# Attention scores as four 64x64 array tiles at a time, mask and row maximum in one VectorE instruction, strided heads first, k loads from ScalarE's queue

## The chip, the cores and the metric

The kernel runs on one core of one Trainium2 chip. The metric is the device time of one execution in microseconds. The kernel before takes 834.89 us (median of three runs, 834.66 to 837.99).

## The reference, cut to what matters

Three layers follow each other. Banded attention over 4 batches, 8 heads, 576 positions and 64 channels gives 2304 rows of 512 numbers; a mixture of 8 experts (top 1) works on these rows; a rational-function feed-forward layer ends it. The change is in the attention alone:

```python
scores = scale * np.matmul(q, k.transpose(0, 1, 3, 2))
mask_plain = (rel >= 0) & (rel < window)                                            # heads 0 to 3, window 32
mask_dil = (rel >= 0) & (rel < window * dilation) & (rel % dilation == 0)           # heads 4 to 7, dilation 4
scores = np.where(masks[None, :, :, :], scores, -1000000000.0)
scores = scores - np.max(scores, axis=-1, keepdims=True)
attn = np.exp(scores)
attn = attn / (np.sum(attn, axis=-1, keepdims=True) + 1e-09)
return np.matmul(attn, v)
```

## The kernel before, in words

A unit is one head of two batches; there are 16, two to a chunk, four chunks to a pair of batches (`CHUNKS`). `KINDS` says which chunks are plain heads (0) and which are strided (1): plain first in the first pair of batches, strided first in the second. The strided heads are stored with their positions sorted by remainder of 4, so that both kinds have the same band. A unit is cut into 9 blocks of 64 queries, and a block meets 96 keys. Four consecutive blocks make a group; the 36 groups are the turns of the loop in `fused`, and the code of a turn is issued by hand in this order: a piece of a later unit's transposes (`qk_T`), the scores of group g (`step_s`), the exponentials of group g-1 (`step_e`), the transposes of group g-2 (`step_t`), another piece of `qk_T`, the product with v of group g-3 (`step_v`), and one gate task (transposes and a small product for the expert logits). Every engine works in the order of issue.

- `load` (L421) brings q and k of a chunk on SP's queue, `load_values` (L439) v, `halo` (L467) copies the last 32 rows of each block to the next on GpSimd.
- `qk_T` (L471) transposes q and k on TensorE to channels x positions (tile `pq`). ScalarE takes k out (`kT`). q is taken out in two halves of 64 partitions, one by ScalarE and one by VectorE (`evac`, L504 and L506), into `qT`, which has zeros beside each half: queries of the two batches stand in one 128-row weight matrix as a block diagonal, in stripes of 16.
- `preset` (L511) fills the score tile `sc` in PSUM with the mask, on TensorE for the first two groups (L516), on ScalarE after them (L518). `step_s` (L520) adds four 128x128 by 128x96 products to it (L525), and VectorE takes the row maxima of all four blocks in one instruction (`mx`, L528).
- `step_e` (L531) takes four exponentials from PSUM (L535). `step_t` (L538) transposes them on TensorE (`pt`, L542), and VectorE copies them out and undoes the stripes (`pts`, L544). `step_v` (L548) multiplies by v in eight 96x64 products (`pv`, L555); VectorE forms the sums' reciprocals and scales (`rs`, `xu`, L560 to L569).
- `spin` (L664) issues matmuls of zeros; `SPIN` says how many stand before each piece of the first unit's transposes. `idle` is their tile.
- After the loop come the last groups' steps, routing, the experts and the last layer, which the change leaves alone.

Of the kernel before, what the change touches and what calls it, by code (L numbers as in the profile page):

```python
# [8 lines left out]
F32 = mybir.dt.float32  # L9
# [13 lines left out]
NJ = S // QT  # L23
# [9 lines left out]
KINDS = ((0, 0, 1, 1), (1, 1, 0, 0))  # L33
# [12 lines left out]
def band_mask(kind, j):  # L46
# [4 lines left out]
    if kind:  # L51
# [4 lines left out]
MASK_SEQ = ([(0, j) for j in (1, 1, 1, 1, 0, 1, 1, 1)] + [(1, j) for j in range(NJ)] + [(1, j) for j in (0, 1, 2, 6, 7, 8)]  # L56
            + [(0, j) for j in (0, 1, 1)])


def mask_start(g):  # L60
    want = []
    for i in range(TPG):
        u, j = divmod(TPG * g + i, NJ)
        kind = CHUNKS[u // 2][2]
        want.append((kind, j if kind else min(j, 1)))
    for s in range(len(MASK_SEQ) - TPG + 1):
        if MASK_SEQ[s:s + TPG] == want:
            return s
    raise AssertionError(want)


def band_masks():
    m = np.stack([band_mask(k, j) for k, j in MASK_SEQ])
    n = m.shape[0]
    m = np.broadcast_to(m.reshape(n, QT // CQ, 1, CQ, KT), (n, QT // CQ, 2, CQ, KT)).reshape(n, 128, KT)
    return np.ascontiguousarray(m.transpose(1, 0, 2))
# [14 lines left out]
SPIN = (13, 0, 4, 0, 6)  # L91
# [82 lines left out]
def fused(ctx, tc, io):  # L174
# [38 lines left out]
    identb = early.tile([128, 128], BF16, name="identb")  # L213
    nc.vector.tensor_copy(out=identb, in_=ident)
# [33 lines left out]
    nc.scalar.activation(out=warm, in_=warm, func=AF.Exp)  # L248
# [144 lines left out]
    with ExitStack() as actx, tc.manual_schedule(), nc.allow_low_precision(reason="integers"):  # L393
# [11 lines left out]
        ps_s = sctx.enter_context(tc.tile_pool(name="ps_s", bufs=2, space=PSUM, side="right"))  # L405
# [5 lines left out]
        qTs = [keep.tile([128, S // CQ, 2, CQ], F32, name=f"qT{i}") for i in range(NB)]  # L411
        mask = keep.tile([128, len(MASK_SEQ), KT], BF16, name="mask")
# [5 lines left out]
        def load(c):  # L418
            bp, _, kind, h0 = CHUNKS[c]
            raw[c] = []  # L420
            for nm, src in (("q", q), ("k", k)):  # L421
                if kind:
                    t = ld.tile([72, 2, 2, 8 * D], F32, tag="ld" + nm, name="ld" + nm)
                    for bb in range(2):
                        nc.sync.dma_start(out=t[:, :, bb, :],
                                          in_=src[2 * bp + bb, h0:h0 + 2].rearrange("h (p j) d -> p h (j d)", j=8))
                else:
                    t = ld.tile([QT, 2 * NJ, 2, D], F32, tag="ld" + nm, name="ld" + nm)
                    if c > 0:
                        load_head(t, src, bp, h0, 2)  # L430
                raw[c].append(t)
# [13 lines left out]

        def load_head(t, src, bp, h0, n):
            for bb in range(2):
                nc.sync.dma_start(out=t[:, 0:NJ * n, bb, :], in_=src[2 * bp + bb, h0:h0 + n].rearrange("h (j a) d -> a (h j) d", a=QT))
# [22 lines left out]
        def qk_T(u, part):  # L471
# [3 lines left out]
            p = ps_q.tile([128, 5 * QT], F32, tag="pq", name="pq")  # L475
            if CHUNKS[c][2]:
                bb = half
                for jj in range(4):
                    nc.tensor.transpose(p[:, 72 * jj:72 * jj + 72], src[:, hh, bb, 128 * jj:128 * jj + 128], ident[0:72, 0:72])
# [196 lines left out]
        for g in range(NG):  # L676
# [13 lines left out]
            if g < NG:  # L690
                if g < 2:
                    preset(g)
# [982 lines left out]
```

## Time and profile before

| | |
|---|---|
| Median of the runs | 834.89 us |
| The profiled execution | 835.69 us, span 833.9 us |
| TensorE busy over the span | 807.4 us (97%) |
| VectorE, ScalarE, GpSimd busy | 584.5, 520.4, 152.3 us |
| Mean granted TensorE clock | 0.973 |
| Scores of the first, fourth and last group begin on TensorE | 10.27, 18.73, 135.88 us |

A busy share says how long an engine had some instruction in it, and TensorE's share is high because matmuls overlap and their ends are modelled. What a stage costs is seen in the chain of waits, which walks back from the last instruction to whatever released it, and in the distance from one group's scores to the next group's. The granted clock is a share of 2.4 GHz: 1.00 is that, 0.50 is 1.2 GHz.

### The profile page before, as it was taken

Reading aid. Unit: us, or ns where it says so; the run is one execution under the profiler, and the core shown is the slowest. Engines: PE = TensorE matmul, PEld = TensorE weight load, DVE = VectorE, ACT = ScalarE, POOL = GpSimd, SP = SyncE. Lnnn points to the kernel's source line nnn. Section 1 sums busy time; section 2 is a strip of 40 time slices with the busy share of each in tenths; the row PEclk is TensorE's granted clock in tenths of the full one; section 3 lists DMA queues with packets and bytes.
Section 4 is the critical chain, followed back from the end, with each engine's and each line's share of the span. In section 5 each row is a group of like instructions: output and inputs, shape, how many; then the busy total and the mean of one; then the engine's idle time right before and its main releaser. Section 6 shows DMA issues by size and latency. Waiting matters only on the chain.

```text
span 833.9 us, 14403 instructions
## 1 busy us (share of the span) xinstructions
PE 807.4 (97%) x4994; PEld 663.2 (80%) x4994; DVE 584.5 (70%) x1151; ACT 520.4 (62%) x1027; POOL 152.3 (18%) x194
## 2 busy tenths in 40 slices
PE   7999999799999999999989999999999999999996
PEld 5888877587876688888868888888888888999894
DVE  3578787860522253796389988888888888888884
ACT  4468666523432344564498977776786778778783
POOL 2211015630101001132075421200020002001001
PEclk9589999999999999999999999999999999999999
DMA  9847884378668756785110000200010001001000
GB/s 158 197 111 182 140 189 138 76 271 286 203 230 297 286 207 248 256 284 185 32 38 27 26 0 13 77 13 0 1 64 25 1 1 64 1 0 39 2 1 38
DMA packets 73569, 91.87 MB, mean 110 GB/s; under 512 B 33641, under 2 KB 43259, under 8 KB 73467
## 3 DMA queue, kind: packets, MB, share of 16 engines
q1 hardware_dynamic: 69051, 77.54, 32.3%
q0 software_dynamic: 3360, 11.03, 3.8%
q10 hardware_dynamic: 1056, 2.10, 0.7%
q8 instruction: 46, 0.75, 0.4%
q14 instruction: 56, 0.46, 0.2%
HBM read 75.94 MB, written 14.71 MB: 109 GB/s over the span
## 4 chain that ended last, share of the span: by engine, by line
PE 86%; DMA 5%; DVE 4%; ACT 2%; SPq 1%; issue 1%; POOL 0%; POOLq 0%
PE p1t L1406 8%; PE p1t L1407 7%; PE p1t L1408 7%; PE sc L525 4%; DMA sw<-in_w 4%; PE p1t L153 4%; PE p1t L155 4%; PE p1t L157 4%; PE pht L1577 3%; PE pht L1576 3%; PE pht L1578 3%; PE pot L820 3%; PE pot L818 3%; PE pot L822 3%; PE pv L555 3%; PE pot L1578 2%
## 5 line engine op out<-in xcount | busy, mean ns | idle before, releaser
L1524 ACT ACTIVATE raw<-p1t 128x512 f32<-128x512 f32 (+1 forms) x78 | 43.1, 553 | 81.9 <-PE p1t L1408 77.4
L1531 DVE TENSOR_TENSOR raw<-raw,raw 128x512 f32<-128x512 f32 (+1 forms) x80 | 51.9, 649 | 59.1 <-ACT raw L1525 58.6
L811 DVE TENSOR_TENSOR hl<-pht,hh 128x512 fp32r<-128x512 f32 x34 | 21.9, 686 | 96.8 <-ACT hh L810 96.5
L1408 PE MATMUL p1t<-yh,wl 128*128 128x512 f32 (+1 forms) x240 | 89.0, 371 | 0.0
L1587 POOL DMA_INDIRECT out<-hs,row x10 | 10.9, 1088 | 301.4 <-ACT hs L1585 300.0
L1525 ACT ACTIVATE raw<-raw,bab 128x512 f32<-128x512 f32 (+1 forms) x80 | 61.9, 773 | 3.0 <-ACT raw L1524 0.4
L1406 PE MATMUL p1t<-yh,wh 128*128 128x512 f32 (+1 forms) x160 | 59.6, 372 | 0.3 <-DVE m L1542 0.3
L1407 PE MATMUL p1t<-yl,wh 128*128 128x512 f32 (+1 forms) x160 | 59.2, 370 | 0.0
L1553 DVE SCALAR_TENSOR_TENSOR m<-m,nab,raw 128x512 f32<-128x512 f32 (+1 forms) x80 | 58.7, 733 | 0.1
L153 PE MATMUL p1t<-w1h,xh 128*128 128x512 f32 x144 | 57.8, 401 | 0.3 <-ACT xh L145 0.2
L157 PE MATMUL p1t<-w1h,xl 128*128 128x512 f32 x144 | 56.6, 393 | 0.0
L155 PE MATMUL p1t<-w1l,xh 128*128 128x512 f32 x144 | 56.5, 392 | 0.0
L1551 DVE SCALAR_TENSOR_TENSOR raw<-raw,raw 128x512 f32<-128x512 f32 (+1 forms) x80 | 56.4, 705 | 0.0
L1526 ACT ACTIVATE raw<-p1t,nab 128x512 f32<-128x512 f32 (+1 forms) x78 | 56.0, 718 | 0.0
L1533 ACT ACTIVATE raw<-raw,bab 128x512 f32<-128x512 f32 (+1 forms) x80 | 53.7, 672 | 0.5 <-DVE raw L1531 0.4
L1542 DVE SCALAR_TENSOR_TENSOR m<-m,nab,p1t 128x512 f32<-128x512 f32 (+1 forms) x78 | 53.5, 686 | 0.1
L1549 DVE SCALAR_TENSOR_TENSOR raw<-raw,raw 128x512 f32<-128x512 f32 (+1 forms) x80 | 51.6, 645 | 0.0
L818 PE MATMUL pot<-w2h,hh 128*128 128x512 f32 x128 | 51.5, 403 | 0.0
L1540 DVE TENSOR_TENSOR m<-raw,p1t 128x512 f32<-128x512 f32 (+1 forms) x78 | 49.3, 632 | 2.7
L820 PE MATMUL pot<-w2l,hh 128*128 128x512 f32 x128 | 51.0, 398 | 0.0
L1408 PEld LDWEIGHTS p1t<-yh,wl 128*128 128x128 f32 x240 | 45.0, 188 | 6.6 <-POOL wl L1459 0.3
L822 PE MATMUL pot<-w2h,hl 128*128 128x512 f32 x128 | 50.2, 392 | 0.0
(380 smaller groups left out, 2157.5 us busy)
## 6 DMA issues: line engine op xcount, KB each, us to landing
sw<-in_w SPq DMA_DIRECT2D x80, 256.0 KB
raw<-in_w SPq DMA_DIRECT2D x10, 1024.0 KB
dr<-in_w_in SPq DMA_DIRECT2D x16, 512.0 KB
dr<-in_w_out SPq DMA_DIRECT2D x16, 512.0 KB
y<-ys_rows SPq DMA_DIRECT2D x18, 256.5 KB
ys_rows<-yo SPq DMA_DIRECT2D x17, 256.5 KB
ldq<-in_q SPq DMA_DIRECT2D x14, 288.0 KB
ldk<-in_k SPq DMA_DIRECT2D x14, 288.0 KB
```

The source lines that it names most:

```text
L153: nc.tensor.matmul(out=p, lhsT=xh[:, kk], rhs=wh[n][:, kk], start=(kk == 0), stop=False)
L155: nc.tensor.matmul(out=p, lhsT=xh[:, kk], rhs=wl[n][:, kk], start=False, stop=False)
L157: nc.tensor.matmul(out=p, lhsT=xl[:, kk], rhs=wh[n][:, kk], start=False, stop=(kk == 3))
L818: nc.tensor.matmul(out=p, lhsT=a[:, c], rhs=w2h[n][:, kk], start=(c == 0), stop=False)
L820: nc.tensor.matmul(out=p, lhsT=a[:, c], rhs=w2l[n][:, kk], start=False, stop=False)
L822: nc.tensor.matmul(out=p, lhsT=b[:, c], rhs=w2h[n][:, kk], start=False, stop=(c == 7))
L1406: nc.tensor.matmul(out=p[:, 0:n], lhsT=wh(kk)[:, cs], rhs=ab[0][:, kk, 0:n], start=(kk == 0), stop=False)
L1407: nc.tensor.matmul(out=p[:, 0:n], lhsT=wh(kk)[:, cs], rhs=ab[1][:, kk, 0:n], start=False, stop=False)
L1408: nc.tensor.matmul(out=p[:, 0:n], lhsT=wl(kk)[:, cs], rhs=ab[0][:, kk, 0:n], start=False, stop=(kk == 3))
L1525: nc.scalar.activation(out=v, in_=ah, func=AF.Identity, scale=bab[:, 1:2], bias=bab[:, 0:1])
L1551: nc.vector.scalar_tensor_tensor(out=v, in0=v, scalar=2.0, in1=r, op0=ALU.subtract, op1=ALU.mult)
L1553: nc.vector.scalar_tensor_tensor(out=m, in0=m, scalar=nab[:, 0:1], in1=v, op0=ALU.add, op1=ALU.mult)
```

## The change

- `KINDS` puts the strided chunks first in both pairs of batches.
- Scores: no block diagonal and no stripes any more. A group is eight products of 64 channels by 64 queries by 96 keys; `i % 2` picks the upper or lower half of the output partitions, `b` (the batch) the half of the input partitions and one of two PSUM banks. So each product uses a quarter of the array, and four in a row use four different quarters. Each 128x96 piece of a bank then holds two neighbouring blocks of one batch.
- The mask is not put into PSUM. `mask` now holds one 128x96 pattern for each pair of blocks that occurs (12 instead of 26 entries), and `tensor_tensor_reduce` on VectorE adds it, changes the sign, writes the result to SBUF (`pe`) and gives the row maximum's negative, one instruction for each 128x96 piece; the exponential reads `pe` in SBUF and turns the sign back. `preset`, `identb` and their instructions go.
- q comes out of PSUM in one ScalarE instruction on 128 partitions; VectorE has no part in it. `qT` needs no zeros, so three GpSimd memsets go. The copy `pts` and the product with v index the new layout.
- The score tile's pool has one buffer of two banks instead of two of one bank.
- First loads: q on SP's queue, k and the first nine mask patterns on ScalarE's queue. Since chunk 0 is strided now, its twelve v loads come before chunk 1's q and k on SP's queue. The warm-up exponential of ScalarE is issued after its loads.
- `SPIN` changes, and three spins follow the scores in each of the first three groups.

```diff
-KINDS = ((0, 0, 1, 1), (1, 1, 0, 0))
+KINDS = ((1, 1, 0, 0), (1, 1, 0, 0))
-SPIN = (13, 0, 4, 0, 6)
+SPIN = (12, 0, 1, 0)
...
-        ps_s = sctx.enter_context(tc.tile_pool(name="ps_s", bufs=2, space=PSUM, side="right"))
+        ps_s = sctx.enter_context(tc.tile_pool(name="ps_s", bufs=1, space=PSUM, side="right"))
...
             if c == 0:
                 for hh in range(2):
-                    for t, src in zip(raw[0], (q, k)):
-                        load_head(t[:, NJ * hh:], src, bp, hh, 1)
+                    for t, src, eng in zip(raw[c], (q, k), (nc.sync, nc.scalar)):
+                        eng.dma_start(out=t[:, hh], in_=src[bs, h0 + hh].rearrange("b (p j) d -> p b (j d)", j=8))
                     if hh == 0:
-                        nc.sync.dma_start(out=mask[:, 0:8], in_=io["mask"][:, 0:8])
+                        nc.scalar.dma_start(out=mask[:, 0:NP0], in_=io["mask"][:, 0:NP0])
+                return
...
-        def preset(g):
-            t = sc[g] = ps_s.tile([128, TPG, KT], F32, tag="sc", name="sc")
...
-            if g < 2:
-                nc.tensor.matmul(out=t, lhsT=identb, rhs=m, start=True, stop=False, skip_group_check=True)
-            else:
-                nc.scalar.activation(out=t, in_=m, func=AF.Copy)
-
         def step_s(g):
-            t = sc[g]
+            t = ps_s.tile([128, 2, 512], F32, tag="sc", name="sc")
+            pe = wk.tile([128, TPG, KT], F32, tag="pe", name="pe")
+            mx = wk.tile([128, TPG], F32, tag="mx", name="mx")
             for i in range(TPG):
-                u, j = divmod(f0 + i, NJ)
-                nc.tensor.matmul(out=t[:, i, :], lhsT=qTs[u % NB][:, 4 * j:4 * j + 4].rearrange("p n b a -> p (n b a)"),
-                                 rhs=kTs[u % NB][:, QT * j:QT * j + KT], start=False, stop=True, skip_group_check=True)
-            mx = wk.tile([128, TPG], F32, tag="mx", name="mx")
-            nc.vector.tensor_reduce(out=mx, in_=t, op=ALU.max, axis=AX.X, negate=True)
+                u, j = divmod(TPG * g + i, NJ)
+                rs, cs = slice(64 * (i % 2), 64 * (i % 2) + 64), slice(KT * (i // 2), KT * (i // 2) + KT)
+                for b in range(2):
+                    ds = slice(64 * b, 64 * b + 64)
+                    nc.tensor.matmul(out=t[rs, b, cs], lhsT=qTs[u % NB][ds, QT * j:QT * j + QT], rhs=kTs[u % NB][ds, QT * j:QT * j + KT],
+                                     start=True, stop=True, skip_group_check=True)
+            for i in range(TPG):
+                b, pair = divmod(i, 2)
+                nc.vector.tensor_tensor_reduce(out=pe[:, i], in0=t[:, b, KT * pair:KT * pair + KT], in1=mask[:, PATTERNS.index(PAIRS[2 * g + pair])],
+                                               scale=-1.0, scalar=3.0e38, op0=ALU.add, op1=ALU.min, accum_out=mx[:, i:i + 1])
...
-                nc.scalar.activation(out=pe[:, i, :], in_=t[:, i, :], func=AF.Exp, bias=mx[:, i:i + 1])
+                nc.scalar.activation(out=pe[:, i, :], in_=pe[:, i, :], func=AF.Exp, bias=mx[:, i:i + 1], scale=-1.0)
...
-                if g < 2:
-                    preset(g)
                 step_s(g)
+            if g < 3:
+                spin(3)
```

On SP, from the start of the program, the kernel before issues this (`ldq` and `ldk` are q and k as loaded, `vw` is v):

```order
L198 DMA ident<-in_cst 128x128
L448 DMA ldq<-in_q 64x9x64 x2
L448 DMA ldk<-in_k 64x9x64 x2
L437 DMA mask<-in_mask 128x768
L448 DMA ldq<-in_q 64x9x64 x2
```

and the changed kernel this, up to chunk 1's q:

```order
L191 DMA ident<-in_cst 128x128
L415 DMA ldq<-in_q 72x2x512 x2
L442 DMA vw_152<-in_v 64x4x128 x2
L442 DMA vw_152<-in_v 16x4x128 [waits DMAHW0_49]
L442 DMA vw_152<-in_v 48x4x128 [waits DMAHW1_49]
...
L442 DMA vw_152<-in_v 64x4x128 [waits DMAHW1_49]
L423 DMA ldq<-in_q 72x2x512 [waits DMAHW2_49]
```

Chunk 1's q has twelve v loads ahead of it instead of the other k, mask and two v loads, and chunk 0's k and the mask have left this queue. The last v load and chunk 1's q wait for a DMA semaphore that an earlier load set.

On TensorE in the third, fourth and fifth turn of the loop, where chunk 1's q is first used, the kernel before has:

```order
L525 MATMUL sc<-kT_149,qT_152 128x96 x3
L542 MATMUL pt<-ident,pe 96x128 x4
L494 MATMUL pq<-ident,ldq 128x64 x5
L525 MATMUL sc<-kT_149,qT_152 128x96 x4
L542 MATMUL pt<-ident,pe 96x128 x4
L494 MATMUL pq<-ident,ldq 128x64 x4
L555 MATMUL pv<-vw_155,pts 64x65 x8
```

and the changed kernel:

```order
L485 MATMUL sc<-kT_146,qT_149 64x96 x6
L626 LDWEIGHTS blank
L626 MATMUL idle<-blank 128x512
...
L503 MATMUL pt<-ident,pe 96x128 x4
L463 MATMUL pq<-ident,ldq 128x72 x4
L485 MATMUL sc<-kT_146,qT_149 64x96 x8
L503 MATMUL pt<-ident,pe 96x128 x4
L463 MATMUL pq<-ident,ldq 128x72 x4
L515 MATMUL pv<-vw_152,pts 64x65 x8
```

The order of the steps is the same; a group's scores are eight small products for four large ones, and spins stand behind the scores of the first three groups.

On VectorE one group of the kernel before is:

```order
L504 TENSOR_SCALAR qT_152<-pq 64x18x16
L528 TENSOR_REDUCE mx<-sc 128x4
L544 COPY pts<-pt 96x512
L504 TENSOR_SCALAR qT_152<-pq 64x18x16
L560 TENSOR_SCALAR rs<-pv 64x4 x2
L561 RECIPROCAL rs<-rs 128x4
```

and of the changed kernel:

```order
L489 ISA pe,mx<-sc,mask 128x96
L489 ISA mx 128x1
...
L505 COPY pts<-pt 96x512
L520 TENSOR_SCALAR rs<-pv 64x4 x2
L521 RECIPROCAL rs<-rs 128x4
L529 TENSOR_TENSOR xu<-pv,rs 128x4x64
```

The one maximum has become four pairs of instructions, each a masked piece and the reading of its minimum, and the two pieces of q are gone.

## Rows read from the trace of the kernel before

**Rows 1.** Windows by stage: stretch, length, busy PE, PEld, DVE, ACT, POOL, clock, DMA, GB/s.
```profile
0.00:18.00 18.00, 13.72 (x89) 8.42 (x89) 5.97 (x20) 7.26 (x20) 5.56 (x12) 1.00 1.10 159
18.00:49.20 31.20, 31.16 (x226) 27.73 (x227) 15.57 (x46) 13.82 (x44) 7.67 (x13) 0.51 0.79 167
49.20:96.40 47.20, 46.88 (x586) 40.67 (x583) 39.08 (x116) 34.96 (x112) 3.96 (x4) 1.00 0.68 148
96.40:137.00 40.60, 40.22 (x471) 32.87 (x469) 32.55 (x107) 27.43 (x83) 6.29 (x7) 1.00 0.68 139
137.00:146.00 9.00, 7.15 (x89) 5.50 (x89) 7.63 (x23) 6.18 (x17) 8.49 (x9) 0.81 0.84 279
```
**Rows 2.** Chain that ended last, attention: start us, us, engine tile line.
```profile
11.34 6.56 DMA ldq<-in_q
18.80 1.95 PE sc L525 x8
...
49.68 0.91 PE sc L525 x8
...
52.63 0.91 PE sc L525 x8
...
57.29 0.62 PE pv L555 x16
...
100.48 1.06 PE sc L525 x8
...
103.92 1.06 PE sc L525 x8
```
**Rows 3.** TensorE's timeline: start us, us, line, tile, forms, idle before and its end.
```profile
1.20 4.44 PE L666 MATMUL idle<-blank 128*128 128x512 bf16 x13 [1.20 <-DVE lg L247]
...
18.04 0.76 PE L494 MATMUL pq<-ident,ldq 64*128 64x64 f32 x5 [2.44 <-DMA ldq<-in_q]
...
49.52 0.74 PE L525 MATMUL sc<-kT,qT 128*128 128x96 f32 x5
...
135.88 1.03 PE L525 MATMUL sc<-kT,qT 128*128 128x96 f32 x8
...
140.69 1.13 PE L555 MATMUL pv<-vw,pts 96*64 96x65 f32 x16 [1.85 <-DVE pts L544]
```
**Rows 4.** SP's queue: two loads in time order; below, durations of one load line.
```profile
9.47 3.16 SPq L448 DMA_DIRECT2D ldq<-in_q  x2
...
L458 SPq DMA_DIRECT2D vw<-in_v x24: 311/592/2303, 27.9 to 71.2; - x24
```
**Rows 5.** Windows, the fastest stretch of DMA; columns as in rows 1.
```profile
180.00:200.00 20.00, 20.00 (x109) 16.32 (x111) 4.41 (x15) 5.92 (x11) 4.09 (x11) 1.00 0.97 353
```
**Rows 6.** Groups by form, 0 to 340 us: busy us, mean ns, idle before.
```profile
L544 DVE COPY pts<-pt 96x512 f32<-96x512 f32 x36 | 24.4, 678 | 1.8 <-PE pt L542 1.8
...
L528 DVE TENSOR_REDUCE mx<-sc 128x4 f32<-128x384 f32 x36 | 20.1, 557 | 17.3 <-PE sc L525 15.1 <-ACT pe L535 1.5
...
L518 ACT ACTIVATE sc<-mask 128x384 f32<-128x384 bf16 x34 | 16.8, 494 | 1.1
...
L560 DVE TENSOR_SCALAR rs<-pv 64x4 f32<-64x4 f32 x72 | 11.4, 159 | 7.5 <-PE pv L555 6.7
...
L504 DVE TENSOR_SCALAR qT<-pq 64x288 f32<-64x288 f32 x16 | 7.4, 461 | 2.5 <-ACT qT L506 1.7
...
L561 DVE RECIPROCAL rs<-rs 128x4 f32<-128x4 f32 x36 | 6.4, 178 | 1.2
```
**Rows 7.** VectorE's timeline, one group and one small instruction.
```profile
104.48 0.49 DVE L569 TENSOR_TENSOR xu<-pv,rs 128x128 f32<-128x128 f32 x2
105.02 0.56 DVE L528 TENSOR_REDUCE mx<-sc 128x4 f32<-128x384 f32 x1
105.49 0.68 DVE L544 COPY pts<-pt 96x512 f32<-96x512 f32 x1
...
111.59 0.15 DVE L346 TENSOR_SCALAR hole<-m 128x1 f32<-128x1 f32 x1
```

More of the change, by code (lines that the diff above doesn't have):

```diff
@@ L53, in band_mask, with block @@
     return np.where(ok, 0.0, -1.0e9).astype(np.float32)
[L56 to L69, printed above, removed]
+def block(f):
+    u, j = divmod(f, NJ)
+    kind = CHUNKS[u // 2][2]
+    return kind, j if kind else min(j, 1)
+PAIRS = [(block(f), block(f + 1)) for f in range(0, 2 * len(CHUNKS) * NJ, 2)]
+PATTERNS = list(dict.fromkeys(PAIRS))
+NP0 = 9
 def band_masks():
-    m = np.stack([band_mask(k, j) for k, j in MASK_SEQ])
-    n = m.shape[0]
-    m = np.broadcast_to(m.reshape(n, QT // CQ, 1, CQ, KT), (n, QT // CQ, 2, CQ, KT)).reshape(n, 128, KT)
+    m = np.stack([np.concatenate([band_mask(*b) for b in pair]) for pair in PATTERNS])
     return np.ascontiguousarray(m.transpose(1, 0, 2))
@@ L410, in fused @@
         kTs = [keep.tile([128, WIN + S], F32, name=f"kT{i}") for i in range(NB)]
-        qTs = [keep.tile([128, S // CQ, 2, CQ], F32, name=f"qT{i}") for i in range(NB)]
-        mask = keep.tile([128, len(MASK_SEQ), KT], BF16, name="mask")
+        qTs = [keep.tile([128, S], F32, name=f"qT{i}") for i in range(NB)]
+        mask = keep.tile([128, len(PATTERNS), KT], BF16, name="mask")
         vws = [keep.tile([KT, 4, NJ, 2 * D + 2], F32, name=f"vw{i}") for i in range(2)]
@@ L495, in qk_T @@
-            if which:
-                nc.scalar.activation(out=kTs[u % NB][:, WIN + j0 * QT:WIN + j1 * QT], in_=p[:, 0:n * QT], func=AF.Copy)
-                return
-            for bb in range(2):
-                hp = slice(64 * bb, 64 * bb + 64)
-                evac(bb, qTs[u % NB][hp, 4 * j0:4 * j1, bb, :], p[hp, 0:n * QT].rearrange("p (n a) -> p n a", a=CQ))
-        def evac(on_dve, o, i):
-            if on_dve:
-                nc.vector.tensor_scalar(out=o, in0=i, scalar1=0.125, scalar2=None, op0=ALU.mult)
-            else:
-                nc.scalar.activation(out=o, in_=i, func=AF.Copy, scale=0.125)
+                    nc.tensor.transpose(p[:, 72 * jj:72 * jj + 72], src[:, hh, half, 128 * jj:128 * jj + 128], ident[0:72, 0:72])
@@ new lines, in qk_T @@
+                i = p[:, 0:288].rearrange("p (c r n) -> p r n c", c=2, r=2)
+                o = dst[:, 288 * half:288 * half + 288].rearrange("p (r n c) -> p r n c", r=2, c=2)
+            else:
+                j0, j1 = ((0, 5), (5, 9))[half]
+                for j in range(j0, j1):
+                    nc.tensor.transpose(p[:, QT * (j - j0):QT * (j - j0 + 1)], src[:, hh * NJ + j].rearrange("p b d -> p (b d)"), ident[0:QT, 0:QT])
+                i, o = p[:, 0:(j1 - j0) * QT], dst[:, j0 * QT:j1 * QT]
@@ L508, in fused @@
+            nc.scalar.activation(out=o, in_=i, func=AF.Copy, scale=1.0 if which else 0.125)
         NG = NU * NJ // TPG
         sc, pex, pts, xus = {}, {}, {}, {}
[L511 to L518 removed]
@@ L543, in step_t @@
             pt = wk.tile([KT, TPG, 128], F32, tag="pts", name="pts")
[L544 to L545 removed]
+            nc.vector.tensor_copy(out=pt, in_=p)
             pts[g] = pt
@@ L654, in fused @@
         load(0)
+        nc.scalar.activation(out=warm, in_=warm, func=AF.Exp)
         load_values(0)
@@ L659, in fused @@
         halo(1)
-        nc.sync.dma_start(out=mask[:, 8:], in_=io["mask"][:, 8:])
+        nc.sync.dma_start(out=mask[:, NP0:], in_=io["mask"][:, NP0:])
         small_loads()
```

63 lines of the change are left out of this document (14 added, 49 removed).

## The prediction

> **What bounds the kernel now.** I read the windows by stage first. The first 137 us are attention, and TensorE is busy in nearly all of three of its four stretches, while VectorE is busy for 83% and 80% of the two later ones [rows 1]. So TensorE is ahead, but VectorE is not far behind. The same rows show a second bound: from 18.0 to 49.2 us TensorE has a clock of 0.51, its lower level of 1.2 GHz, and 1.00 before and after. The chain of waits agrees: it is TensorE work from 18.04 us on, and before that the load of a q tile [rows 2, 3]. The timeline then shows why the clock fell: TensorE stood idle for 2.44 us until chunk 1's q had landed, and went on at the lower level [rows 3]. A later idle time of 1.85 us has the clock at 0.81 over its stretch of 9 us [rows 1, 3]. Once down, the clock stayed down for 31 us of full busy time, six groups of scores (from 18.80 to 49.52 us, 5.12 us each). The 26 groups from 49.52 to 135.88 us took 3.32 us each at the higher level [rows 2, 3].
>
> After attention the change touches nothing, and what follows starts from its end. So I price attention alone, and take what it gains or loses as the kernel's.
>
> **The change part by part.** The sum is made against the profiled execution's 835.69 us; the median of the runs is 0.8 us lower.
>
> *Scores on TensorE.* Now eight instructions of a group take 0.91 us, 0.114 us each, and 1.06 us where 64-row transposes stand ahead of them [rows 2]. So a change of the array's shape costs about 0.15 us. The changed group has sixteen instructions (each fp32 product shows as two), on 64-column weights and 96 moving columns. The nearest row is `pv`: sixteen instructions, 64-column weights, 65 moving columns, two column halves in turn, in 0.62 us, a change of shape included [rows 2, 3]. Without that change it is 0.47 us for sixteen, and 0.47 x 96/65 = 0.69 us for 96 columns if only the two column halves run beside each other; half of it, 0.35 us, if the row halves do too. I take the middle, 0.52 us. The shape now differs from that of the transposes ahead and behind, so two changes are added, 0.30 us: 0.82 us (0.65 to 0.99). That is 0.09 us less than 0.91 in strided stretches and 0.24 less than 1.06 in plain ones, and from 0.41 us gained to 0.08 lost at the ends.
>
> The row for this is the 0.91 against 1.06 us of [rows 2]. The Trainium skill's TensorEngine Tiling (Array Packing), § Key Properties, says that changing the tiling mode drains TensorE; the trace agrees, at 0.15 us. By its table of theoretical speedups the scores would go to a quarter of their time, and the sum would be some 15 us lower; `pv` does not bear that out.
>
> *VectorE.* One group costs it now, by starts: scaling 0.54 us, the maximum 0.47, the copy about 0.65 [rows 7], two sums 0.32 and a reciprocal 0.21 with their gaps, and q's halves, 0.46 us each, 32 of them in 36 groups, 0.41 [rows 6]. That is 2.60 us. The maximum and q go: 1.72 us stay. What comes is four pairs, a 96-element piece and the reading of its result. The trace has no such instruction. From below: two pieces of 128 elements in 0.54 us are 0.27 each, less 0.04 for 32 elements fewer (0.47 us for 384 elements are 1.2 ns each), with the read hidden: 0.23. From above: the piece runs to its end, 0.25 us by the same count, and a small instruction in full, 0.15, follows [rows 7]: 0.40. I take 0.30, nearer to the row of back-to-back pieces: 1.20 us, and 2.9 us for the group (2.6 to 3.3). So VectorE and TensorE come out about even in strided stretches (TensorE: 2.95 us from 49.68 to 52.63 us, less 0.09), and TensorE leads in plain ones (3.44 us from 100.48 to 103.92 us, less 0.24, is 3.2) [rows 2].
>
> *ScalarE and GpSimd.* 34 presets of 0.494 us go [rows 6]; ScalarE was never what the chain waited for in this stretch, so that is worth nothing. q's second half costs it nothing, since an instruction on 128 partitions replaces one on 64 of the same length. Three memsets on GpSimd go at a time when nobody waits for it.
>
> *The one score buffer.* Group g+1's scores now wait until VectorE has read group g's. Behind that wait stand the transposes `pt` and `pv` on TensorE. From a group's scores to their last reading is 0.82 + 1.20 us, 2.0, less than the 2.9 us to the next group, so it costs nothing while VectorE is on time.
>
> *The start.* Twelve spins of 0.34 us from 1.20 us on [rows 3] reach 5.3 us; the first unit's transposes and their evacuation take two more, and three groups of about 2 us each (scores, three spins, VectorE's reading), then `pt`: TensorE asks for chunk 1's q at about 13.8 us. That load is issued behind fifteen others, twelve of them v loads of about 0.59 us [rows 4], so at about 9 us, as before (9.47). With itself 3.2 MB go by then: chunk 0's q and k 1.18, v 1.18, mask and identity 0.28, its own 0.59. At 159 GB/s, the rate of this stretch [rows 1], they take 20 us; at 353, the best stretch [rows 5], 9 us, and with its issue at 9 it would land at some 11. The pieces that a descriptor moves are 512 B and 2 KB long instead of 256 B, so I take the middle, 15 us, and the fourth group's scores at 15.5 us instead of 18.80: -3.3 us (-5 to +2). The idle time is then about 1.2 us, under the 1.85 us that cost the clock.
>
> *The clock.* If it stays up, the six groups that took 30.7 us take 3.1 us each, 18.6: -12.1 us (-13.5 to 0).
>
> *The 26 later groups.* Fourteen strided ones at about 0.05 us (VectorE's 2.9 us against 2.95) and twelve plain ones at 0.24: -3.6 us (-8 to +2).
>
> *The end.* The last group's reading costs 1.20 for 0.47 us in the chain: +0.7 us.
>
> Sum: -3.3 - 12.1 - 3.6 + 0.7 = -18.3 us, so 817.4 us for an execution like the profiled one and 816.5 us for the median.
>
> **The rivals.**
>
> *The clock falls as before.* Chunk 1's q lands two microseconds later than I think, TensorE idles for more than 1.85 us, and six groups or so run at 1.2 GHz. For it speaks that a 2.44 us wait did just that [rows 3] and that the q load has more v loads ahead of it; against it the larger packets and the nine added spins. The scores' row there is 1.95 us; twice 0.82 is 1.64, so a group gains 0.3 us: -2 instead of -12, and the start -1.5. Then -6.4 us: 829.
>
> *The clock falls and stays down.* This is the slower one. What lifted it at 49 us is not clear from busy time, which was full for all 31 us [rows 1]. Small score products may do less to lift it. A group at the lower level costs 4.8 us against 3.1: 1.7 us lost per group. With 18 us won elsewhere, it decides from 11 such groups on; after all 32 groups 54 us are lost and 18 won, 871. Against it: the same gate tasks as before follow from the eighth group on.
>
> *VectorE takes the bound.* If a pair costs 0.40 us, a group is 3.3 us everywhere, and 32 of them take 106 us: the last group's scores begin at 121 instead of 135.88 us, and with the end's 0.7 us some 14 us are gained: 821. VectorE's 83% is the sign for it [rows 1]. The Trainium skill's TensorEngine Tiling (Array Packing), § PSUM Bottleneck, has the rule: tiling speeds up TensorE, not the emptying of PSUM, which may become the bound. By that rule 821; the trace so far has VectorE second.
>
> *The quarters don't run beside each other.* Then sixteen instructions follow each other at 0.085 us (0.114 x 96/128, if the 128 weight columns set it now and the 96 moving ones then), 1.36 + 0.30 us, +0.7 us a group over the present 0.95, and 32 groups of 4.0 us end at 143 us instead of 136: 842. The two column halves of `pv` speak against it.
>
> **How the numbers follow.** Chances: forecast 0.48, clock falls as before 0.24, VectorE bounds 0.13, clock stays down 0.10, no parallel quarters 0.05. About 0.5%, 4.2 us, is what can be told from no change. Faster by more: 0.48 + 0.19 + 0.12 = 0.79; within: 0.05 of the first rival, 0.01 of the third, 0.02 of the second, 0.08; slower: 0.08 + 0.05 = 0.13. The range of the forecast alone is 809 (start -5, clock -13.5, later groups -8, end +0.7: -25.8) to 823; with the first and third rivals it is 809 to 832.
>
> **What would show it.** Granted clock 1.00 from 18 to 49 us; the fourth group's scores at about 15.5 us and the last group's at about 116; eight score products in 0.5 us and more before the transposes behind them start; a pair on VectorE from start to start near 0.30 us; VectorE over 95% busy in strided groups. A clock of 0.5 after the first wait, or pairs of 0.4 us, would make me wrong in the size; a last group's scores after 140 us in the sign.

## The result, and the profile after

The changed kernel takes 822.57 us (median of four runs, 820.0 to 826.8) against 834.89 us: a ratio of 0.9849, 95% interval 0.98 to 0.9897. It is 1.5% faster. Here and below, an interval compares the runs within 1.5% of the fastest of their kernel, while medians and ranges hold all runs, so that an interval can lie beside the ratio of the medians (in the set of e9 and e10, one run of before at 822.22 us takes ten of its 23 out). The time is inside the range of 809 to 832 us and six microseconds above the 816.5 us forecast. The profiled execution is the slowest of the four, 826.8 us with a span of 825.0; before had 835.69 and 833.9. Of these 8.9 us, the terms of the prediction make up:

| term (by starts of scores on TensorE) | before | after | measured | forecast |
|---|---|---|---|---|
| fourth group begins | 18.73 | 18.09 | -0.6 | -3.3 |
| the six groups from there | 30.8 us | 18.7 us | -12.1 | -12.1 |
| 26 later groups, to the last group's start | 86.4 us | 88.6 us | +2.2 | -3.6 |
| from there to the end of the span | 698.0 us | 699.6 us | +1.6 | +0.7 |

The windows by stage of the changed kernel (columns as in rows 1) show where the clock went:

```profile
11.00:15.00 4.00, 3.84 (x35) 2.56 (x33) 1.60 (x16) 1.88 (x6) 0.00 (x0) 0.57 0.60 156
15.00:18.00 3.00, 2.17 (x31) 1.55 (x30) 1.49 (x9) 1.47 (x5) 2.90 (x3) 1.00 0.86 238
18.00:49.20 31.20, 28.70 (x465) 21.74 (x463) 24.13 (x141) 19.91 (x64) 4.38 (x6) 1.00 1.14 176
72.00:96.40 24.40, 22.15 (x265) 16.62 (x266) 14.12 (x78) 12.23 (x37) 3.73 (x5) 0.72 1.11 183
96.40:127.00 30.60, 29.39 (x451) 21.17 (x449) 26.00 (x142) 18.88 (x60) 5.71 (x7) 1.00 0.65 144
```

From 18.0 to 49.2 us the clock is 1.00 where it was 0.51 [rows 1]. It was low once before that, 0.57 from 11 to 15 us, and came back. But from 72 to 96 us, where before had 1.00, it is now 0.72. TensorE's timeline says what stood ahead of that (columns as in rows 3):

```profile
10.10 0.44 PE L463 MATMUL pq<-ident,ldq 72*128 72x72 f32 x4 [1.48 <-DMA ldq<-in_q]
...
17.70 0.47 PE L463 MATMUL pq<-ident,ldq 72*128 72x72 f32 x4 [0.67 <-DMA ldq<-in_q]
18.09 0.56 PE L485 MATMUL sc<-kT,qT 64*64 64x96 f32 x16
...
29.35 0.49 PE L469 MATMUL pq<-ident,ldq 64*128 64x64 f32 x5 [0.86 <-DMA ldq<-in_q]
...
33.41 0.50 PE L469 MATMUL pq<-ident,ldk 64*128 64x64 f32 x5 [1.02 <-ACT bab L254]
...
73.65 0.47 PE L463 MATMUL pq<-ident,ldq 72*128 72x72 f32 x4 [1.22 <-DMA ldq<-in_q]
```

The wait of 2.44 us at 18 us [rows 3] is 0.67 us now. A new wait for a q tile has come at 72.4 us. The four groups from 74.05 us took 18.65 us together; where the clock stayed up (experiments below) the same four took 12.5. The group that holds the wait, from 70.20 us, took 3.85 us. The chain of waits of the changed kernel, from 69.5 us (start, us, what), has a second load of the same q, which landed at 75.37 us:

```profile
69.52 0.15 SPq L423
...
69.72 5.65 DMA ldq<-in_q
...
75.42 0.47 PE pq L463 x4
```

and SP's queue (start, us, line, loads or stores in time order) shows what stood ahead of this load and of chunk 1's:

```profile
2.08 11.75 SPq L442 DMA_DIRECT2D vw<-in_v  x12
13.87 1.01 SPq L423 DMA_DIRECT2D ldq<-in_q  x2
...
45.34 7.91 SPq L605 DMA_DIRECT2D x_rows<-xu  x8
...
54.59 4.28 SPq L605 DMA_DIRECT2D x_rows<-xu  x8
...
59.63 9.42 SPq L442 DMA_DIRECT2D vw<-in_v  x12
69.14 0.96 SPq L423 DMA_DIRECT2D ldq<-in_q  x2
```

Chunk 5's q (69.14 us) stands behind twelve strided v loads and twenty stores of the first pair's results, which the new order of heads puts into one piece at 44.67 to 59.5 us. In the kernel before, this q was issued later still, at 72.67 us, but TensorE came to it at 86.05 us and found it there; now TensorE is ready for it at 72.4.

Chunk 1's q was issued at 13.87 us and not at 9, because the twelve v loads took 11.75 us. The chain from 9 to 20 us has the price of one of them, and the load of chunk 0's k that SP had waited for:

```profile
1.86 8.95 DMA ldk<-in_k
...
10.82 0.59 SPq L442
```

A v load costs 0.59 us, as the prediction had it, and twelve are 7.1 us. The rest is waiting for earlier loads, 4.9 us by the list of waits of that queue from 0 to 20 us (who waited for what: us in total, times, longest):

```profile
SPq L442 <- DMA ldq<-in_q: 2.7, 2, 1.9
SPq L442 <- DMA ldk<-in_k: 2.2, 2, 1.7
```

The shorter groups are there. The changed kernel on TensorE, one plain group:

```profile
46.22 0.56 PE L485 MATMUL sc<-kT,qT 64*64 64x96 f32 x16
46.71 0.64 PE L503 MATMUL pt<-ident,pe 128*96 128x128 f32 x4
...
49.22 0.40 PE L485 MATMUL sc<-kT,qT 64*64 64x96 f32 x8
```

Scores take 0.49 us from their start to the transposes behind them, and the group 3.00 us to the next group's scores, against 3.44 before. Strided groups take 2.66 us (64.83 to 67.50 us) against 2.95 [rows 2]. And VectorE in a strided group, with the windows' row for 60 to 72 us behind it (for rows of before, [rows 6, 7]):

```profile
65.57 0.26 DVE L489 CUSTOM_DVE_ANT_0 pe<-sc,mask 128x96 f32<-128x96 f32 x1 [0.35 <-ACT qT L471]
65.75 0.09 DVE L489 DVE_READ_ACCUMULATOR2_ANT mx<- 128x1 f32 x1
65.75 0.25 DVE L489 CUSTOM_DVE_ANT_0 pe<-sc,mask 128x96 f32<-128x96 f32 x1
...
67.46 0.49 DVE L529 TENSOR_TENSOR xu<-pv,rs 128x192 f32<-128x192 f32 x2
```
```profile
60.00:72.00 12.00, 12.00 (x212) 9.85 (x209) 10.36 (x64) 8.87 (x31) 1.24 (x2) 1.00 0.49 131
```

A piece runs 0.25 us, but the next begins 0.18 us after it, and the 0.08 us reading starts together with the next piece, so it costs nothing. VectorE is busy for 10.36 of 12 us, 86%, and waits a little in each group; TensorE is busy for all of it.

### The profile page after: what moved, and what is told of

Same layout as the page of the kernel before. It is cut to its first block, busy times and chain, and to the rows that moved or that the text cites. A ratio compares the mean times of both kernels' runs of the same rounds, so it can differ in the third digit from the quotient of the medians.

```text
span 825.0 us, 15207 instructions
## 1 busy us (share of the span) xinstructions
PE 791.3 (96%) x5277; PEld 638.4 (77%) x5279; DVE 577.6 (70%) x1370; ACT 509.7 (62%) x993; POOL 149.0 (18%) x191
## 4 chain that ended last, share of the span: by engine, by line
PE 83%; DMA 8%; DVE 4%; ACT 3%; issue 1%; SPq 0%; POOL 0%; POOLq 0%; ACTq 0%; DVEq 0%
PE p1t L1363 8%; PE p1t L1364 8%; PE p1t L1365 8%; DMA sw<-in_w 5%; PE p1t L146 4%; PE p1t L150 4%; PE p1t L148 4%; PE pht L1533 4%; PE pht L1534 3%; PE pht L1535 3%; PE pot L777 3%; PE pot L775 3%; PE pot L779 3%; PE pot L1535 2%; PE pxt L1533 2%; PE pxt L1534 2%
## 5 line engine op out<-in xcount | busy, mean ns | idle before, releaser
L489 DVE CUSTOM_DVE_ANT_0 pe<-sc,mask 128x96 f32<-128x96 f32 x144 | 28.4, 253 | 31.6 <-PE sc L485 19.6
```

## The experiments

The kernel before was run beside each of them; its median was 834.1 to 835.6 us in the four sets. "Six groups" are those from the fourth on, all starts are from one profiled execution each, and its clock need not be that of the median run.

| kernel | median us (range) | 95% interval of the ratio to before | six groups | 26 later | last scores at |
|---|---|---|---|---|---|
| before | 834.89 | | 30.8 | 86.4 | 135.9 |
| changed | 822.57 (820.0-826.8) | 0.98-0.9897 | 18.7 | 88.6 | 125.4 |
| e1 old scores | 824.9 (822.2-827.0) | 0.9861-0.9936 | 17.8 | 88.4 | 124.9 |
| e2 new scores alone | 825.17 (821.1-830.0) | 0.9858-0.9926 | 27.0 | 84.1 | 129.5 |
| e3 stores spread | 825.84 (815.9-830.2) | 0.9805-0.9919 | 27.0 | 85.3 | 130.8 |
| e4 loads moved | 831.91 (822.9-835.4) | 0.9903-0.9977 | 29.2 | 85.9 | 133.7 |
| e5 no spins | 828.52 (821.7-844.6) | 0.9896-0.997 | 27.1 | 85.4 | 130.9 |
| e7 = e3, start filled | 820.25 (815.7-829.5) | 0.9744-0.9882 | 18.3 | 80.6 | 116.6 |
| e8 = e7, small products later | 817.95 (814.4-822.1) | 0.9746-0.9841 | 22.0 | 85.3 | 125.3 |
| e9 = e8, five spins | 821.56 (819.0-829.4) | 0.9857-0.995 | 18.9 | 80.4 | 117.4 |
| e10 start filled only | 826.67 (822.5-831.5) | 0.9896-0.9985 | 17.5 | 91.8 | 127.7 |
| e12 = e8, six spins | 821.22 (818.3-825.4) | 0.9786-0.9881 | 18.0 | 82.6 | 118.9 |

**One part at a time: e1 and e2.** e1 has before's scores with the changed order of heads, loads and spins:

```diff
-KINDS = ((0, 0, 1, 1), (1, 1, 0, 0))
+KINDS = ((1, 1, 0, 0), (1, 1, 0, 0))
-SPIN = (13, 0, 4, 0, 6)
+SPIN = (12, 0, 1, 0)
...
+                    for t, src, eng in zip(raw[c], (q, k), (nc.sync, nc.scalar)):
```

> The old scores (block diagonal, mask in PSUM, one row maximum a group, q taken out by two engines) with the new order of heads, the new first loads and the new spins. My theory: the change gains in two separate parts, the clock at its upper level from about 15 us on instead of 48.6 (some 12 us) and shorter groups (2.66 for 2.95 us strided, 3.00 for 3.44 plain), and gives half of it back in waits for q loads. Then this kernel has the first part alone: groups of 2.95 and 3.44 us at full clock, 821 to 826 us in all. Rival: the clock is kept by the scores' own shape; then the old scores fall to 1.2 GHz behind the first wait here too, and it is 832 us or more.

e2 has the changed kernel's scores with before's order, loads and spins:

```diff
-KINDS = ((1, 1, 0, 0), (1, 1, 0, 0))
+KINDS = ((0, 0, 1, 1), (1, 1, 0, 0))
-SPIN = (12, 0, 1, 0)
+SPIN = (13, 0, 4, 0, 6)
```

> The new scores (four array quarters, masked maximum on VectorE) with the old order of heads, the old first loads and the old spins. My theory: the clock falls behind chunk 1's wait near 18 us as in the kernel before and stays down for six groups or so, but each group is shorter, by 0.3 us strided, 0.44 plain and some 0.7 at the low clock: 26 x 0.36 + 6 x 0.7 = 13.5 us, 820 to 825 us. Rival: the scores are off the path (VectorE bounds the groups), all gain is from the start and the clock: 833 to 836 us.

Measured: 824.9 and 825.17 us, each some 10.5 us under the 835.59 of before in their set and about what was expected. The windows of e1 and then of e2, 18 to 49.2 us, tell the two gains apart:

```profile
18.00:49.20 31.20, 31.17 (x373) 26.48 (x373) 25.99 (x78) 22.90 (x74) 5.16 (x7) 1.00 1.10 178
```
```profile
18.00:49.20 31.20, 31.20 (x320) 25.09 (x319) 18.50 (x95) 14.08 (x45) 7.65 (x13) 0.50 0.75 160
```

e1 keeps the clock at 1.00 with the old groups; which of its parts (order of heads, loads, spins) does it, e1 can't say. e2 loses it as before does, behind a wait of 2.27 us for chunk 1's q:

```profile
17.70 0.76 PE L471 MATMUL pq<-ident,ldq 64*128 64x64 f32 x5 [2.27 <-DMA ldq<-in_q]
```

It gains by shorter groups instead. So the clock at the start is worth about 10.5 us, the new scores about 10.5 us, and if the two were independent, both at once would give 21; the changed kernel gets 12.3. Some 9 us are missing, and the profiles show two reasons of about 10 us together. The four groups behind the wait at 72 us lose 6.2 (18.65 us for 12.5). And the two gains overlap: 3.8 us of e2's were made in the six groups at the lower clock (27.0 us for 30.8), and with the clock up the new scores gain nothing there (e1 17.8 us, changed 18.7 with its waits at 29 and 33 us).

The clock gain can also be seen without any change. Four of the 73 runs of before in these sets had a mean clock of 0.988 or 0.989, and took 822.2 to 827.8 us, as e1's six did (822.2 to 827.0 at 0.983 to 0.989). What e1 changes is how often the clock stays up. At like clocks the new scores are worth some 6 us: of all runs at 0.988 or more, the eight with the old scores (before, e1) have a median of 824.4 us, the 19 with the new ones (e3, e7 to e10, e12) one of 818.7.

e1 on TensorE also shows what the scores themselves are worth in a plain group:

```profile
47.10 1.13 PE L526 MATMUL sc<-kT,qT 128*128 128x96 f32 x8
48.07 0.60 PE L543 MATMUL pt<-ident,pe 128*96 128x128 f32 x4
...
50.53 1.28 PE L526 MATMUL sc<-kT,qT 128*128 128x96 f32 x8
```

0.97 us to the transposes against 0.49, and 3.43 us for the group against 3.00: the group's gain is the scores' own.

**The wait at 72 us: e3.** The first pair's twenty stores are issued three per turn, from the thirteenth turn on and after the v loads:

```diff
+            def store(out, in_):
+                if c == 0:
+                    stores.append(lambda: nc.sync.dma_start(out=out, in_=in_))
+                else:
+                    nc.sync.dma_start(out=out, in_=in_)
...
+            for _ in range(3):
+                if stores and g > 11:
+                    stores.pop(0)()
```

> The changed kernel with one difference: the 20 stores of the first pair's strided rows are issued three to a turn after the v loads, instead of all at once ahead of them on SP's queue. My theory: the wait for chunk 5's q at 72 us, and the fall of the clock from 76 to 90 us behind it, come from these 20 stores standing ahead of it on that queue. Then both go, groups 21 to 24 take 2.7 to 3 us instead of 3.9 to 5.5, and the time falls by 6 to 9 us, to 813 to 817 us. Rival: the clock falls in this stretch because TensorE's work has become thin, whatever the queue: 820 to 824 us, as the changed kernel.

A miss: 825.84 us. In e3's timeline chunk 5's q is not waited for, and the four groups behind it took 12.5 us instead of 18.65:

```profile
18.09 0.47 PE L463 MATMUL pq<-ident,ldq 72*128 72x72 f32 x4 [3.08 <-DMA ldq<-in_q]
...
84.63 0.41 PE L463 MATMUL pq<-ident,ldq 72*128 72x72 f32 x4
```

That doesn't show yet that the stores had caused the wait, since TensorE came to this q 11 us later than in the changed kernel; e7 and e10 below settle it. The median did not fall. In this execution the wait for chunk 1's q at 15 to 18 us, the same load, was 3.08 us, and the clock from 18 to 49 us 0.51. In the changed kernel's own profile the clock was low from 11 to 15 us, TensorE came late to that load, and so waited 0.67 us. The six runs lie between 815.85 us (clock 0.989) and 830.19 (0.964): whether the clock falls at the start differs from run to run.

**The load itself earlier: e4.** To e3, chunk 1's q and k ahead of the v loads, and the two `small_work` pieces three and two turns later:

```diff
-        load_values(0)
-        halo(0)
         load(1)
+        load_values(0)
+        halo(0)
...
-            if g in (7, 10):
-                small_work(ps_q, g == 10)
+            if g in (10, 12):
+                small_work(ps_q, g == 12)
```

> As the kernel with the stores spread, and chunk 1's q and k are issued before chunk 0's twelve v loads, and the small preparation that waits for the last small load comes three turns later. My theory: the 0.67 us wait at 17.7 us and the 1.02 us wait at 33.4 us go, so 1 to 3 us less than the kernel with the stores spread: 811 to 815 us. Rival: v is then late instead, and the first product with v waits about as long: no difference.

831.91 us: not less, and the theory fell. It is 6 us above e3's median, with intervals that overlap a little. The rival had the wait right and its price wrong: now v is late, by as much as q was (timeline of e4), and the clock is 0.58 from 18 to 49 us.

```profile
23.24 0.92 PE L515 MATMUL pv<-vw,pts 96*64 96x65 f32 x12 [3.05 <-POOL vw L453]
```

Chunk 1's q and chunk 0's v are in one queue, and in both orders tried TensorE waited some 3 us for the one that stood last.

**The spins behind the scores: e5.**

```diff
-            if g < 3:
-                spin(3)
```

> The changed kernel without the three spins behind the scores of the first three groups. My theory: whether the clock stays up is settled by how long TensorE stands idle before chunk 1's q, which lands at about 18 us; without the nine spins TensorE is there 2 us earlier, idles 3 us or more in every execution, and runs at 1.2 GHz for ten groups: 826 to 831 us, granted clock 0.965 to 0.97. Rival: the nine spins keep nothing up and only cost time: 820 to 823 us.

828.52 us, the time expected, but not by the path expected. The wait for chunk 1's q is 1.73 us and not 3 or more, and the clock, 0.50 from 18 to 49.2 us, had fallen long before it (timeline and window of e5):

```profile
17.80 0.74 PE L463 MATMUL pq<-ident,ldq 72*128 72x72 f32 x4 [1.73 <-DMA ldq<-in_q]
```
```profile
15.00:18.00 3.00, 1.27 (x10) 0.83 (x7) 1.49 (x9) 0.30 (x2) 2.95 (x4) 0.50 0.77 211
```

From 11 to 15 us it was 0.51 in e5 and 0.57 in the changed kernel, behind waits of 1.76 and 1.48 us for chunk 0's q at 10 us. With the nine spins it came back before 18 us, without them it did not. In the other profiles with the spins in which it fell there, it came back in e1, e4 and e6, and stayed low in e11.

**The four quarters: e6 and e11.** e6 issues the eight products so that neighbours share a quarter:

```diff
-            for i in range(TPG):
-                u, j = divmod(TPG * g + i, NJ)
+            for b in range(2):
+                for i in (0, 2, 1, 3):
+                    u, j = divmod(TPG * g + i, NJ)
...
-                for b in range(2):
```

> The changed kernel with the same eight products of a group in another order: batch by batch, and in a batch first the two of one output half, then the two of the other, so that neighbours share rows or a whole quarter of the array. My theory: the 0.49 us of a group's scores come from four quarters at work beside each other; here two neighbours at most can, and the scores take 0.7 to 1.0 us. Rival: the array takes the products one after the other and 0.49 us is what 64-column weights cost: no change in the 0.49 us.

One run, 822.58 us, and the scores took 0.51 us, not 0.7 to 1.0:

```profile
39.44 0.58 PE L485 MATMUL sc<-kT,qT 64*64 64x96 f32 x16
39.95 0.64 PE L503 MATMUL pt<-ident,pe 128*96 128x128 f32 x4
```

The order hardly matters, so this run could not say whether the quarters work in parallel. e11 takes two of them away:

```diff
-lhsT=qTs[u % NB][ds, QT * j:QT * j + QT], rhs=kTs[u % NB][ds, QT * j:QT * j + KT],
+lhsT=qTs[u % NB][0:64, QT * j:QT * j + QT], rhs=kTs[u % NB][0:64, QT * j:QT * j + KT],
```

> The changed kernel with both batches' products taken from the first batch's 64 input channels, so that a group's sixteen instructions use only the two quarters of the upper input half; the second batch's scores are wrong. If all four quarters work beside each other, sixteen instructions now take twice as long, about 0.7 us from the scores to the transposes behind them instead of 0.49 us, and the kernel loses up to 0.2 us a group. If the row halves don't run beside each other anyway, the scores stay at 0.49 us.

TensorE's timeline of e11, one strided group at full clock:

```profile
83.30 0.93 PE L485 MATMUL sc<-kT,qT 64*64 64x96 f32 x16
84.16 0.64 PE L503 MATMUL pt<-ident,pe 128*96 128x128 f32 x4
...
86.33 0.87 PE L485 MATMUL sc<-kT,qT 64*64 64x96 f32 x15
```

The same sixteen instructions take 0.86 us on two quarters and 0.49 on four, and the group 3.03 us instead of 2.66. So the two input halves work beside each other; e11 leaves both output halves in use, and that these do so too rests on `pv` of the kernel before, sixteen instructions on the two output halves in 0.62 us [rows 2]; one after the other they would take 1.2 us, an estimate from 0.114 us for 96 columns on the whole array. The median (848.57 us, 836.87 to 852.47) can't be set against the others, since in its profile the clock is low from 11 to 62 us.

**The start filled: e7, e8 and e10.** To e3, spins where TensorE would wait at the start:

```diff
-SPIN = (12, 0, 1, 0)
+SPIN = (16, 0, 1, 0)
...
+        spin(5)
         done_T, done_L = 4, 2
...
+            if g == 2:
+                spin(12)
             qt(1)
```

> As the kernel with the stores spread, with spins where TensorE waited for loads: four more before the first transposes, five before the loop, twelve before the transposes of chunk 1's q, which lands at about 18 us anyway. My theory: the clock then stays up in nearly every execution (granted clock 0.985 or more), the two gains of the change add up, and it is 813 to 817 us, below both kernels; groups 3 to 11 take 2.4 to 3.8 us instead of 4.1 to 5.3. Rival: the clock falls behind another wait, at 29 or 33 us, or the products are too thin for it: 820 to 826 us.

e8 is e7 with the later `small_work` of e4's diff.

> As the kernel with the wait filled by spins, and the small preparation that waits for the last small load comes three turns later, so that ScalarE is not held at 32 to 33 us. My theory: the 1.0 us wait of TensorE for ScalarE there goes: 0.5 to 1 us less, 812 to 816 us. Rival: another wait, for chunk 2's k, takes its place: no difference.

In e7's profile (windows) the clock is up through both stretches and the last scores begin at 116.56 us:

```profile
18.00:49.20 31.20, 28.85 (x474) 21.84 (x466) 24.25 (x141) 20.49 (x67) 5.48 (x11) 1.00 1.07 177
49.20:96.40 47.20, 46.45 (x760) 35.86 (x753) 37.95 (x225) 32.85 (x107) 6.27 (x9) 1.00 0.83 165
```

Three of its runs took 815.7 to 817.2 us (mean clock 0.988 to 0.992), as the theory has it, the three others 823.3 to 829.5 (0.967 to 0.981), and the median, 820.25 us, is the rival's. In all five profiles with the start filled (e7 to e10, e12) the clock is at 1.00 up to 29 us; in the nine others it is low somewhere between 9 and 19 us. e8 has the lowest median, 817.95 us, above the 812 to 816 expected and not to be told from e7's. Its profiled execution is its slowest. It no longer has the wait for ScalarE at 33 us, but lost the clock for some 20 us behind a wait for chunk 2's q:

```profile
29.29 0.62 PE L469 MATMUL pq<-ident,ldq 64*128 64x64 f32 x5 [1.17 <-DMA ldq<-in_q]
```

e10 has e7's start but leaves the stores in one piece (the diff of e7 on the changed kernel).

> The changed kernel with only the start filled: 16 spins for 12, five more before the loop, twelve before the transposes of chunk 1's q; the twenty stores stay in one piece. Theory: the start then keeps its clock, the six groups after the fourth take 19 us as they did, but chunk 5's q is still issued behind the stores, TensorE waits for it at 70 to 73 us, and the clock falls there in most runs: groups 21 to 24 take 4 us and more, median 821 to 824 us, 2 to 4 us above the kernel that also spreads the stores (820.25). Rival (the stores cost nothing, since the wait at 72 us drops the clock only now and then): 818 to 821 us, no different from the one with the stores spread.

826.67 us, higher than expected. Its timeline and windows have the wait of 72 us again, longer, and the clock down behind it:

```profile
73.34 0.47 PE L463 MATMUL pq<-ident,ldq 72*128 72x72 f32 x4 [1.87 <-DMA ldq<-in_q]
```
```profile
72.00:96.40 24.40, 20.80 (x228) 15.73 (x230) 11.52 (x59) 10.49 (x33) 3.86 (x5) 0.65 1.12 182
```

e7, with the stores spread and otherwise the same, came to this q at the same time and did not wait; its SP issued the load at 61.95 us, e10's at 69.08:

```profile
71.36 0.41 PE L463 MATMUL pq<-ident,ldq 72*128 72x72 f32 x4
```

That the stores cause the wait at 72 us is shown by these two. e1 shows the other half of it: with the stores in one piece but the old, longer groups, TensorE came at 75.78 us and did not wait either.

So neither the stores alone (e3) nor the start alone (e10) beats the changed kernel; both together (e7) give 820.25 us, and 816 in the runs that keep the clock. The runs of e7 and e10 overlap, but all four kernels with both parts (e7, e8, e9, e12; 30 runs) have medians of 818.0 to 821.6 us against e10's 826.67.

**The wait at 29 us: e9 and e12.** To e8, five spins in the eighth turn:

```diff
-            if g == 2:
-                spin(12)
+            if g in (2, 7):
+                spin(12 if g == 2 else 5)
```

> The kernel with the stores spread, the start filled and the small products later, plus five spins at the start of the eighth turn, ahead of the first transposes of chunk 2's q, where TensorE waited 1.17 us and then lost the clock for 20 us. My theory (each run loses what one wait at a load costs it in clock): this wait is filled, the clock stays up to 120 us in nearly all runs, the last group's scores begin at 116 to 118 us, median 814 to 817 us, every run under 820. Rival (another short wait drops the clock as often, whichever is filled): the clock is at 0.5 somewhere else in attention in the profile and the median stays at 817 to 821 us.

821.56 us, a miss, and a misplaced edit: the spins stand behind the transposes that wait, as e9's timeline shows.

```profile
29.46 0.49 PE L469 MATMUL pq<-ident,ldq 64*128 64x64 f32 x5 [1.20 <-DMA ldq<-in_q]
...
31.07 1.03 PE L632 MATMUL idle<-blank 128*128 128x512 bf16 x4
```

The wait of 1.20 us was still there, and in this execution the clock stayed up. e12 puts six spins ahead of them:

```diff
+            if g == 7:
+                spin(6)
             qt(1)
             if g < NG:
                 step_s(g)
```

> As the kernel before this one in the series (stores spread, start filled, small products later), but with the spins where the wait really is: the run before put five spins behind the scores of the eighth group, and TensorE still waited 1.20 us for chunk 2's q at 29.46 us, ahead of them. Now six spins stand ahead of those transposes. Theory: the wait at 29 us is gone or under 0.3 us, the clock is 1.00 from 18 to 96 us in the profile, the last group's scores begin at 115 to 118 us, the median is 815 to 818.5 us. Rival (that wait costs the clock too rarely to matter, and the spins only add to TensorE's queue): the median is 819 to 822 us, as in the run with the misplaced spins.

```profile
28.14 1.47 PE L632 MATMUL idle<-blank 128*128 128x512 bf16 x6
29.54 0.52 PE L469 MATMUL pq<-ident,ldq 64*128 64x64 f32 x5
```

The wait is gone and the clock is 1.00 from 18 to 96 us, as the theory said, but the median, 821.22 us, is the rival's: filling this wait brings nothing that can be measured. And the clock fell all the same, later, and with no wait ahead of it (windows of e12; TensorE's timeline from 107 us has no idle time of note):

```profile
110.00:115.00 5.00, 4.95 (x74) 3.55 (x72) 3.24 (x17) 3.24 (x11) 0.00 (x0) 1.00 0.28 59
115.00:118.40 3.40, 3.40 (x39) 2.68 (x40) 2.09 (x13) 0.73 (x2) 2.05 (x2) 0.50 0.12 19
```

Six runs of e8 and six of e12, in different sets, don't show either to be better than the other.

The best version by its median is e8: 0.9793 of before, against 0.9849 for the changed kernel. The intervals overlap, so that it beats before is shown, and that it beats the changed kernel is not.

## Why the prediction was right, and where it was off

**The whole.** The range held, and the largest term, the clock at the start, came about as described. But the profiled execution gained 8.9 us and the median 12.3, for the 18.3 of the sum, so that the range held by its width.

**What bounds the kernel, and the clock.** Right. The wait for chunk 1's q grew short, the clock stayed up behind it in the profiled execution, and the six groups gave the 12.1 us forecast. e1 shows this gain without the new scores. That the size agrees to a tenth is luck: four of the six groups took 2.3 to 3.0 us, less than the 3.1 forecast, and the two others 3.68 and 4.07 us, with waits of 0.86 and 1.02 us at 29 and 33 us that the prediction didn't have. The gain is not safe either: in e3, e5 and e11 the clock fell at the start, with the same loads, in e5 and e11 at 11 us, ahead of the wait that the prediction watched. The forecast gave "the clock falls as before" 0.24; over many runs both happen. "Stays down" was not seen: in each profile the clock is at 0.90 or more from 96.4 to 127 us.

**The start.** The step that failed. The prediction took 0.59 us for a strided v load [rows 4], which holds, and had chunk 1's q issued at 9 us. It put at nothing what SP waits for earlier loads, although the order of instructions shows waits for DMA semaphores: 4.9 us. q was issued at 13.87 us and landed at 17.7, not 15. TensorE was late too, and this kept the wait at 0.67 us: it asked for q at 17.03 and not at 13.8 us, after waits of 1.30 and 1.48 us for chunk 0's q, which the sum left out, and 4 us at a clock of 0.57. -0.6 instead of -3.3 us.

**Scores on TensorE.** Mis-sized in the good direction: 0.49 us, below the low end of 0.65, for the prediction took the middle between two and four parallel quarters. From two quarters (0.86 us) to four, 0.37 us are saved; if work goes by quarters, another 0.37 is work and 0.12 is left for both changes of shape, not 0.30. In strided groups, the scores are 0.42 us shorter and the group only 0.29, since the transposes ahead of the scores take 0.34 us instead of 0.25 (e1) and those behind 0.47 instead of 0.43. The quarter of the time that the prediction names in passing is the wrong measure for this kernel: the block diagonal already took both batches in one product, so eight products on four quarters stand for four on the whole array, and four at a time they take half of the time, 0.49 for 0.97 us. The rival "no parallel quarters" is refuted by e11. The Trainium skill's TensorEngine Tiling (Array Packing), § Key Properties, says that different tiles can load weights and multiply in parallel; these two times agree.

**VectorE.** The pair was mis-sized: 0.18 us, below the bound of 0.23, since the next piece starts while the last is still running. A group costs it some 2.4 us (from 65.57 us to the end of `xu` at 67.95), not 2.9, so "VectorE takes the bound" did not come true: 86% busy, not over 95. The Trainium skill's TensorEngine Tiling (Array Packing), § PSUM Bottleneck, warns that emptying PSUM may become the bound after tiling; the trace has TensorE still ahead in the stretch shown.

**The 26 later groups.** Mis-sized and of the wrong sign, for three reasons that pull apart. By the two steps above, groups gain 0.29 (strided) and 0.44 us (plain) instead of 0.05 and 0.24: with the clock up, the 26 take 80.6 us in e7 and 80.4 in e9, and 88.4 with the old scores in e1. But e1's are also 2.0 us longer than before's 86.4, without the new scores: with strided heads first, some of the strided groups, the short ones (2.95 us against 3.44), now stand ahead of these 26, while the prediction counted fourteen strided and twelve plain ones as in the kernel before. And the changed kernel took 88.6 us, 8 more than e7, of which 7.4 lie in five groups, the one that holds the wait at 72 us and the four behind it. The prediction left that wait out: it followed the first loads of the queue and not those in mid-attention, where TensorE now comes to chunk 5's q 13.6 us earlier than before, and the strided pair's stores stand ahead of it. That this is the cause of the wait is shown by e7 and e10, which differ in the stores alone.

**The end.** +1.6 us against +0.7. In the other profiles this part is 695.0 to 700.3 us, so the difference is within what differs from one execution to the next.

What stays open: what drops the clock in a given run. Waits of 1.17 (e8) and 1.22 us (changed) were followed by a low clock, one of 1.20 us at the same place as e8's was not (e9), and the fall at 115 us in e12 had no wait ahead of it. That filling the start keeps the clock up to 29 us is shown; why it falls is not.

## What to carry to other kernels

When groups get shorter, every load behind them is needed earlier: follow each load queue to the end of the stage, not only to the first wait, and count the stores in it and the waits for earlier loads, which the price of one load does not hold. A wait of a microsecond or two costs little itself, but the lower clock that followed it cost six (changed), eight (e10) and twelve microseconds (before). Gains that were measured apart need not add: one of them may have been made in time that the other takes away. And where a kernel's runs spread with the clock, compare runs at like clocks too.

## What the runs showed of the hardware

- `tensor_tensor_reduce` on 128x96 from PSUM shows as a 0.25 us instruction and a 0.08 us reading, and goes at 0.18 us from start to start.
- Eight 64x64x96 fp32 products take 0.49 us on four quarters of the array and 0.86 us on two; the order in which the quarters follow hardly matters (0.51 us).
- At the lower clock TensorE can be busy for the whole of a stretch of 31 us and stay there (e2: 31.20 of 31.20 us at 0.50), and at the upper one it can fall with TensorE busy for 4.95 of the 5 us ahead (e12).
- SP's queue can stand still for a load issued earlier on another queue: its first twelve v loads took 11.75 us, 4.9 of them waiting, 2.2 of these for k loads from ScalarE's queue.
- A kernel's own runs spread with the clock: e7 from 815.7 us at a mean clock of 0.989 to 829.5 us at 0.967.
